# Top-k attention and a seven-product MLP: the order of fetched and resident products, and where GpSimd's additions are given out

## The chip, the cores and the metric

The kernel runs on one core of one Trainium2 chip. The metric is the device time of one execution in microseconds (us). A core has TensorE (PE, matrix products; PEld is its weight load), VectorE (DVE), ScalarE (ACT), GpSimd (POOL) and SyncE (SP), which here issues nearly all DMA transfers. Each engine has a program of its own and waits for others by semaphores.

## The reference

```python
def _attn_ref(q, k, v):              # B=8, H=8, S=576, D=64, float32
    scores = scale * np.matmul(q, k.transpose(0, 1, 3, 2))
    kth = np.partition(scores, -32, axis=-1)[..., -32:-31]
    scores = np.where(scores >= kth, scores, -1e9)
    attn = np.exp(scores - np.max(scores, axis=-1, keepdims=True))
    attn = attn / (np.sum(attn, axis=-1, keepdims=True) + 1e-09)
    return np.matmul(attn, v)
# bridge: x = attention as (8, 576, 512)
def _moe_ref(x, g_ln, w_ch1, w_ch2): # w_ch1 512 x 2048, w_ch2 2048 x 512
    xn = (x - mean) / np.sqrt(var + 1e-06) * g_ln
    return x + np.maximum(xn @ w_ch1, 0.0) @ w_ch2
```

## The kernel before

**Attention.** Work is cut into 160 *units*: a unit is 128 queries of one pair of heads (or the 64 last queries of both heads, a *rest*). VectorE turns keys and queries (turn_heads, L321), TensorE makes the scores (scores and score_half, L348 to L380), and ACT copies them out of PSUM. VectorE then finds the 32nd largest score of every row in rounds of MAX8 and MATCH_REPLACE8 (select, L404). It does so on two halves: halve (L382) makes the elementwise maximum of the two halves of a row on VectorE (hi) and the minimum on GpSimd by two integer operations (lo, L399 and L402); the first rounds of select read lo. ACT masks (mask, L447) and exponentiates (weigh, L454). The weights are turned for the product with v either by TensorE (turn, L505) or, in 72 *moved* units, by VectorE and two DMA trips through memory (move, L486: two transposes L492, one store L497, four loads L500). values (L563) multiplies with v, place (L590) turns the result into rows of x.

**The MLP.** Two tiles of 128 rows of x make a *block*; there are 18. The first block is computed plainly (plain, L726). The other 17 use seven products of half-size matrices in place of eight for the second layer (seven, L768). A block has three kinds of items: two rows ("turn", L663), 64 hidden products (L700) with a relu on ACT after every eight, and 7 steps of 8 products ("project", L862, matmul L869). The left factors are four parts of the relu's output (part(j, 0) to part(j, 3)) and three sums of them made by GpSimd (sums, L785 to L793). The right factors are either *resident* in SBUF (three quarters of w2) or one of four *forms*: combinations of w2's quarters, computed once (form_pair, L906) and kept in memory. A form is fetched by four DMAs, each a pair of 128x256 pieces (fetch_form, L929, DMA L932), into the four slots that w2's fourth quarter leaves free (slot_of, L903). So a slot of a form is overwritten by the next form's piece once the product that read it is done. The four of the seven steps that use forms are, before, steps 2, 3, 5 and 6.

Each step's bank of PSUM is copied out by ACT when its last product is given out (evacuate, L829, copies L818): four go into the output tile o, three into a tile t from which GpSimd adds them to o (L827). tpool has one buffer for t, and aside (L820) runs everything that is deferred before it takes it. finish (L676) scales o on ACT (L678), adds x on GpSimd (L682) and leaves the store to the next step.

**Order.** Engines execute in the order in which the Python loop at L1126 emits. Its pass n, a *step of the loop*, emits select for unit n, halve for n+1, scores for n+2 and the later stages of units n-1, n-2 and n-3. Between them stand eight calls of fill (L272), which give out block items from the list todo: slot (L1087) spreads the list evenly, so a fill has a share of planned us (0.56 to 0.75 in most of the run, more at the end) and an item has a planned cost (0.4378 us for one product). A call of fill counts the clock tick. defer (L262) puts an action off by some fills: sums by SUM_LAG = 4, joins by 1; settle (L265) runs what is due at the beginning of a fill. After the loop the rest of the list is emitted one item at a time (L1253).

A fetch is emitted by fetch_forms (L939) in a fill, as soon as the product that read its slot was emitted a fill or two ago; forms (L946) emits it on the spot where it is needed and not yet emitted:

```python
    def fetch_forms():
        may = min(seen[0] + 4, 16 * (len(blocks) - 1))
        seen[0] = used[0]
        if done(formed[0]):
            while fetched[0] < may:
                fetch_form()
```

SyncE's queue holds, in order of emission, the stores of finished rows (L684), the forms (L932), the moves (L497, L500), the loads of keys and queries (L299, eight transfers when a new pair of heads is turned), v (L311, L315) and small transfers of denominators (L558).

Of the kernel before, what the change touches and what calls it, by code (L numbers as in the profile page):

```python
# [29 lines left out]
def kernel(  # L30
# [41 lines left out]
    nc = tc.nc  # L72
# [22 lines left out]
    kqpool = pool("kq", 4)  # L95
    vpool = pool("v", NV)
# [162 lines left out]
    pending = []  # L259
    tick = [0]  # L260

    def defer(fills, run):  # L262
        pending.append((tick[0] + fills, run))

    def settle(all_of_them=False):  # L265
        waiting = [x for x in pending if not all_of_them and x[0] > tick[0]]
        due_now = [x for x in pending if all_of_them or x[0] <= tick[0]]
        pending[:] = waiting
        for _, run in due_now:
            run()  # L270

    def fill(least=0):  # L272
        tick[0] += 1
        settle()
        fetch_forms()
        owed[0] = min(owed[0] + share[0], 6.0)
        while todo and (not todo[0][3] or todo[0][3]()):
            if owed[0] < todo[0][1] / 2 and least <= 0:
                break
            least -= 1  # L280
            pop()
# [39 lines left out]
    def turn_heads(job):  # L321
        job.T = {}
        for name in "kq":
            job.T[name] = kqpool.tile([P, S], FP32, tag=name + "T", name=name + "T")
            nc.vector.transpose(job.T[name][:], job.ins[name][:])  # L325
# [32 lines left out]
    def score_half(u, s):  # L358
        T = (u.job.twin or u.job).T
        kT, qT = T["k"], T["q"]  # L360
        q0 = u.qt * P
# [257 lines left out]
    class Block:  # L619
        def __init__(self, tiles, dsts):  # L620
# [5 lines left out]
            self.ready = False  # L626

# [48 lines left out]
        def finish(self, i):  # L676
            o = self.o[i]
            nc.scalar.activation(  # L678
                o[:], o[:], AF.Identity,
                bias=self.mv[:, i, 0:1], scale=self.rstd[:, i : i + 1],  # L680
            )
            nc.gpsimd.tensor_tensor(o[:], o[:], self.x[i], ALU.add)  # L682
            for dst, rows in self.dsts[i]:
                stores.append(lambda d=dst, s=o[rows, :]: nc.sync.dma_start(d, s))  # L684
# [83 lines left out]
        def seven(self):  # L768
# [11 lines left out]
            def run(j, ps):  # L780
                hs[j] = self.relu(ps)
                waiting[j] = True
                defer(SUM_LAG, lambda: sums(j))

            def sums(j):  # L785
                if not waiting.pop(j, False):
                    return
# [10 lines left out]
            def resident(half, side):  # L798
# [3 lines left out]
                ("a", True, lambda j: part(j, 0), resident(0, 0)),  # L802
                ("b", True, lambda j: part(j, 2), resident(1, 0)),
                ("c", True, lambda j: ss[j][:, 0], 0),
                ("a", False, lambda j: ss[j][:, 1], 1),
                ("c", False, lambda j: ss[j][:, 2], resident(1, 1)),
                ("a", False, lambda j: part(j, 1), 2),
                ("d", True, lambda j: part(j, 3), 3),
            )

            def left(i):
                return self.o[i][:, 0:Q]

            def right(i):
                return self.o[i][:, Q:DM]

            def copy(dst, name):
                nc.scalar.copy(dst, bank[name][:, 0:Q])  # L818

            def aside(name, *into):  # L820
                settle(True)
                t = tpool.tile([P, Q], FP32, tag="t", name="t")
                copy(t[:], name)
                return t

            def add(dst, x, y):
                nc.gpsimd.tensor_tensor(dst, x, y, ALU.add)  # L827

            def evacuate(k):  # L829
                if k == 0:  # L830
                    for i in range(2):
                        self.o[i] = opool.tile([P, DM], FP32, tag="o", name="o")
                    copy(left(0), "a")
                elif k == 1:
                    t = aside("b")
                    defer(1, lambda: add(left(0), left(0), t[:]))
                elif k == 2:
                    copy(right(1), "c")
                elif k == 3:
                    copy(right(0), "a")  # L840
                elif k == 4:
# [451 lines left out]
```

## Time and profile before

| what | before |
|---|---|
| time, median of 3 runs | 1752.1 us (1752.0 to 1752.13) |
| the profiled execution, its own time | 1751.76 us |
| its span, first to last instruction | 1749.9 us |
| busy: PE, DVE | 1559.6 us (89%), 1463.3 us (84%) |
| busy: ACT, POOL | 1067.7 us (61%), 971.6 us (56%) |
| granted TensorE clock, mean | 0.950 |
| products L869, TensorE records | 1904, of 400 to 409 ns mean each, overlapping |
| fetches of forms | 272, of 256 KB, median 3.2 us from issue to landing |

A record of a product is half of one[...], so 1904 records are 952 products. Shares of busy time are means over three stretches: until about 300 us the weights are converted beside the first units, until about 1600 us attention and blocks run together, and after that the last blocks run without attention. Waits are listed as waiting instruction <- what released it; line names carry the tile's name and the line in the kernel.

### The profile page before, as it was taken

The numbers are of one execution on the slowest core, as the hardware profiler recorded it, in microseconds if no ns is written. First come the engines' busy times: TensorE is split into PE (matmuls) and PEld (weight loads), VectorE is DVE, ScalarE is ACT, GpSimd is POOL, SyncE is SP. The second block draws the span as 40 slices with busy tenths as digits, with TensorE's granted clock in tenths as the row PEclk, the third lists the DMA queues.
The fourth block names the chain that finished last, engine by engine and source line by source line (L and its number), as shares of the span: only waits on it lengthen the run. The fifth ranks groups of instructions, "written<-read, shape, count | busy, mean of one in ns | idle before, by whom it ended". The sixth has DMA issues, their size and how long they took to land.

```text
span 1749.9 us, 27740 instructions
## 1 busy us (share of the span) xinstructions
PE 1559.6 (89%) x7897; PEld 1146.4 (66%) x7897; DVE 1463.3 (84%) x4620; ACT 1067.7 (61%) x2712; POOL 971.6 (56%) x1509
## 2 busy tenths in 40 slices
PE   2678989999888989899899988989998999999987
PEld 1346556676666766677676766667676667777876
DVE  5998898999899999889899989798989899983000
ACT  6978866676666746566565755656565656653321
POOL 5778678464555646365555554554555455553332
PEclk9879998999899989999999999999999999999999
DMA  6422333413635365355644554535554555443232
GB/s 168 113 91 87 77 97 112 117 34 87 178 111 169 92 171 130 113 150 132 166 142 127 138 148 130 157 100 165 137 164 116 142 133 172 131 122 115 74 90 84
DMA packets 377504, 218.00 MB, mean 125 GB/s; under 512 B 250884, under 2 KB 357384, under 8 KB 377352
## 3 DMA queue, kind: packets, MB, share of 16 engines
q1 hardware_dynamic: 372616, 215.65, 43.9%
q10 hardware_dynamic: 4736, 0.59, 0.3%
q8 instruction: 63, 1.03, 0.2%
q14 instruction: 89, 0.73, 0.1%
HBM read 164.76 MB, written 51.38 MB: 124 GB/s over the span
## 4 chain that ended last, share of the span: by engine, by line
DVE 46%; PE 26%; POOL 10%; DMA 8%; ACT 5%; issue 2%; SPq 2%; DVEq 0%; ACTq 0%; POOLq 0%
DVE m L423 14%; DVE hi L409 12%; PE ops L869 11%; DVE hi L414 7%; PE hps L700 7%; DMA w<-forms 5%; DVE lo L409 4%; DVE hi L394 3%; DVE sc L492 3%; PE scps L373 3%; POOL lo L402 2%; POOL lo L399 2%; PE av L568 2%; DMA turned<-sc 2%; ACT sc L354 1%
## 5 line engine op out<-in xcount | busy, mean ns | idle before, releaser
L700 PE MATMUL hps<-xT,w 128*128 128x256 f32 x2304 | 557.9, 387 | 3.0 <-ACT xT L671 3.0
L423 DVE MAX8 m<-hi 128x8 f32<-128x304 f32 x1152 | 488.4, 460 | 3.3
L700 PEld LDWEIGHTS hps<-xT,w 128*128 128x128 f32 x2304 | 422.8, 193 | 82.5 <-issue 26.4
L409 DVE MATCH_REPLACE8 hi<-m,hi 128x304 f32<-128x304 f32 x864 | 390.2, 458 | 0.0
L399 POOL TENSOR_TENSOR lo<-sc,hi 128x576 int32<-128x576 int32 (+1 forms) x159 | 204.5, 1286 | 270.9 <-DVE hi L394 150.9
L869 PE MATMUL ops<-w,h 128*128 128x256 f32 x1088 | 282.3, 400 | 41.9 <-DMA w<-forms 41.8
L414 DVE MAX8 hi<-lo 128x8 f32<-128x288 f32 x576 | 234.3, 443 | 50.4 <-POOL lo L402 49.1
L869 PEld LDWEIGHTS ops<-w,h 128*128 128x128 f32 x1088 | 203.5, 198 | 90.8 <-DMA w<-forms 50.1
L869 PE MATMUL ops<-w,s 128*128 128x256 f32 x816 | 218.4, 409 | 48.8 <-DMA w<-forms 48.6
L373 PE MATMUL scps<-kT,qT 64*128 64x288 f32 (+3 forms) x1344 | 223.9, 438 | 35.9 <-DVE qT L325 28.3
L354 ACT COPY sc<-scps 128x288 f32<-128x288 f32 x576 | 197.6, 409 | 84.4 <-PE scps L373 56.7
L460 ACT ACTIVATE e<-e,bias 128x576 f32<-128x576 f32 x288 | 225.8, 784 | 14.1 <-POOL bias L445 13.5
L450 ACT ACTIVATE e<-sc,m 128x576 f32<-128x576 f32 x288 | 224.8, 781 | 3.9 <-DVE m L423 3.2
L869 PEld LDWEIGHTS ops<-w,s 128*128 128x128 f32 x816 | 157.1, 204 | 88.2 <-DMA w<-forms 51.9
L402 POOL TENSOR_TENSOR lo<-lo,sc 128x576 int32<-128x576 int32 (+1 forms) x159 | 204.3, 1285 | 12.5
L373 PEld LDWEIGHTS scps<-kT,qT 64*128 64x128 f32 (+1 forms) x1344 | 124.5, 183 | 122.5 <-issue 39.4
L827 POOL TENSOR_TENSOR o<-o,t 128x256 f32<-128x256 f32 x68 | 50.6, 744 | 222.2 <-ACT t L818 136.2
L568 PE MATMUL av<-pt,vb 128*64 128x256 f32 (+2 forms) x1088 | 150.1, 419 | 9.8 <-DMA pt<-turned 5.3
L492 DVE STREAM_TRANSPOSE sc<-e 128x512 f32<-128x512 f32 x144 | 95.0, 688 | 70.1 <-ACT e L460 70.1
L723 ACT ACTIVATE h<-hps 128x512 f32<-128x512 f32 x144 | 86.5, 600 | 71.2 <-PE hps L700 70.4
L409 DVE MATCH_REPLACE8 lo<-hi,lo 128x288 f32<-128x288 f32 x288 | 125.5, 442 | 0.0
L568 PEld LDWEIGHTS av<-pt,vb 128*64 128x64 f32 x1088 | 75.5, 143 | 75.8 <-issue 21.1
(87 smaller groups left out, 1795.8 us busy)
## 6 DMA issues: line engine op xcount, KB each, us to landing
w<-forms SPq DMA_DIRECT2D x272, 256.0 KB, 3.2
turned<-sc SPq DMA_DIRECT2D x72, 512.0 KB, 2.8
pt<-turned SPq DMA_DIRECT2D x288, 128.0 KB, 2.9
vb<-in_v_dram SPq DMA_DIRECT2D x136, 128.0 KB, 2.9
raw<-in_moe_w_ch_dram SPq DMA_DIRECT2D x32, 512.0 KB, 4.1
kin<-in_k_dram SPq DMA_DIRECT2D x128, 72.0 KB, 2.5
qin<-in_q_dram SPq DMA_DIRECT2D x120, 72.0 KB, 2.5
out_dram<-o SPq DMA_DIRECT2D x32, 256.0 KB, 2.9
```

The source lines that it names most:

```text
L354: nc.scalar.copy(u.sc[:, t, s * HALF : (s + 1) * HALF], made[s][t][:, 0:HALF])
L373: nc.tensor.matmul(ps[i * R : i * R + ql, o : o + width], qT[r, q0 : q0 + ql], kT[r, k0 : k0 + width], start=True, stop=True,)
L399: nc.gpsimd.tensor_tensor(lo.bitcast(I32), a.bitcast(I32), hi.bitcast(I32), ALU.subtract)
L402: nc.gpsimd.tensor_tensor(lo.bitcast(I32), lo.bitcast(I32), b.bitcast(I32), ALU.add)
L409: nc.vector.match_replace(x[:, t], m[:, t, :], x[:, t], LOWEST)
L414: nc.vector.max(u.hi[:, t, o : o + 8], u.lo[:, t])
L423: nc.vector.max(m[:, t, :], u.hi[:, t])
L450: nc.scalar.activation(u.e[:, t], u.sc[:, t], AF.Prelu, bias=u.thr[:, t, 7:8], scale=-1.0, alpha=SLOPE)
L460: nc.scalar.activation(u.e[:, t], u.e[:, t], AF.Exp, bias=u.bias[:, t : t + 1], scale=-scale / SLOPE, accum_out=g.den[:, col : col + 1],)
L568: nc.tensor.matmul(av[h * D : (h + 1) * D, 0 : g.nq], vb[:, h * J + c, :], g.blocks[:, h, 0 : g.nq // 32, c, :], start=(c == 0), stop=False,)
L700: nc.tensor.matmul(ps[0][:, side * N : (side + 1) * N], w1[:, c, f * P : (f + 1) * P], self.xT[:, c, 0:N], start=(c == 0), stop=(c == NC - 1),
L869: nc.tensor.matmul(bank[name][:, 0:Q], a(j), rhs, start=first and j == 0, stop=(j == G - 1), skip_group_check=not first,)
```

## The change

- **Steps.** The seven products of a block are put in another order, so that fetched and resident right factors alternate: steps 0, 2, 4 and 6 use forms. The forms are stored in memory in the new order of their use.
- **Fetches.** used becomes a list of the fills in which a slot was last read; a fetch is emitted in a fill once ten fills have passed (FETCH_AGE), or on the spot in forms. All projects of a block wait for formed.
- **GpSimd.** sums, joins and the additions of x go to a list (sums_later) that is settled at one place in a pass of the loop, right behind halve, for entries at least five fills old (SUM_AGE). A product that needs sums which were not yet given out gives them out. The scaling on ACT goes to a second list (ends_later), settled at the beginning of a fill, five fills old (END_AGE). close gives out what a block still has open when the next block's first product is emitted.
- **Buffers.** The three joined results have buffers of their own (tags t3, t5, t6). The last join adds one tile to both halves of o in one operation of 128x512.
- **Queries.** The turned queries are two tiles, of 256 and 320 columns, each with a transpose of its own; the first is in a pool of two buffers.

```diff
@@ -93,6 +93,7 @@
     consts = pool("consts", 1)
     ldpool = pool("ld", 1)
     kqpool = pool("kq", 4)
+    qpool = pool("q", 2)
     vpool = pool("v", NV)
     scpool = pool("sc", 5)
     hipool = pool("hi", 2)
@@ -256,23 +257,36 @@
         owed[0] -= cost
         run()
 
-    pending = []
     tick = [0]
 
-    def defer(fills, run):
-        pending.append((tick[0] + fills, run))
-
-    def settle(all_of_them=False):
-        waiting = [x for x in pending if not all_of_them and x[0] > tick[0]]
-        due_now = [x for x in pending if all_of_them or x[0] <= tick[0]]
-        pending[:] = waiting
-        for _, run in due_now:
-            run()
+    class Later:
+
+
+        def __init__(self):
+            self.waiting = []
+
+        def add(self, run):
+            left = [run]
+
+            def once():
+                if left:
+                    left.pop()()
+
+            self.waiting.append((tick[0], once))
+            return once
+
+        def settle(self, age):
+            due_now = [x for x in self.waiting if tick[0] - x[0] >= age]
+            self.waiting = [x for x in self.waiting if tick[0] - x[0] < age]
+            for _, run in due_now:
+                run()
+
+    sums_later, ends_later = Later(), Later()
 
     def fill(least=0):
         tick[0] += 1
-        settle()
-        fetch_forms()
+        ends_later.settle(END_AGE)
+        fetch_forms(FETCH_AGE)
         owed[0] = min(owed[0] + share[0], 6.0)
         while todo and (not todo[0][3] or todo[0][3]()):
             if owed[0] < todo[0][1] / 2 and least <= 0:
@@ -321,8 +335,13 @@
     def turn_heads(job):
         job.T = {}
         for name in "kq":
-            job.T[name] = kqpool.tile([P, S], FP32, tag=name + "T", name=name + "T")
-            nc.vector.transpose(job.T[name][:], job.ins[name][:])
+            cuts = (0, S) if name == "k" else (0, 2 * P, S)
+            job.T[name] = []
+            for i, (c0, c1) in enumerate(zip(cuts, cuts[1:])):
+                pl = kqpool if c1 == S else qpool
+                t = pl.tile([P, c1 - c0], FP32, tag=f"{name}T{i}", name=name + "T")
+                nc.vector.transpose(t[:], job.ins[name][:, c0:c1])
+                job.T[name].append((c0, t))
 
 
 
@@ -357,8 +376,9 @@
 
     def score_half(u, s):
         T = (u.job.twin or u.job).T
-        kT, qT = T["k"], T["q"]
-        q0 = u.qt * P
+        kT = T["k"][0][1]
+        c0, qT = T["q"][u.qt >= 2]
+        q0 = u.qt * P - c0
         ql = R if u.rest else P
         pss = [brief("scps") for _ in u.tiles]
         for ps, hs in zip(pss, u.tiles):
@@ -624,6 +644,7 @@
             self.mv = None
             self.step = {}
             self.ready = False
+            self.ends = []
 
         def stats(self, i):
             x = self.x[i]
@@ -675,13 +696,20 @@
 
         def finish(self, i):
             o = self.o[i]
-            nc.scalar.activation(
-                o[:], o[:], AF.Identity,
-                bias=self.mv[:, i, 0:1], scale=self.rstd[:, i : i + 1],
-            )
-            nc.gpsimd.tensor_tensor(o[:], o[:], self.x[i], ALU.add)
-            for dst, rows in self.dsts[i]:
-                stores.append(lambda d=dst, s=o[rows, :]: nc.sync.dma_start(d, s))
+
+            def residual():
+                nc.gpsimd.tensor_tensor(o[:], o[:], self.x[i], ALU.add)
+                for dst, rows in self.dsts[i]:
+                    stores.append(lambda d=dst, s=o[rows, :]: nc.sync.dma_start(d, s))
+
+            def scaled():
+                nc.scalar.activation(
+                    o[:], o[:], AF.Identity,
+                    bias=self.mv[:, i, 0:1], scale=self.rstd[:, i : i + 1],
+                )
+                self.ends.append(sums_later.add(residual))
+
+            self.ends.append(ends_later.add(scaled))
 
         def rows(self):
             return [
@@ -779,12 +807,9 @@
 
             def run(j, ps):
                 hs[j] = self.relu(ps)
-                waiting[j] = True
-                defer(SUM_LAG, lambda: sums(j))
+                waiting[j] = sums_later.add(lambda: sums(j))
 
             def sums(j):
-                if not waiting.pop(j, False):
-                    return
                 a11, a21, a12, a22 = (hs[j][:, i * P : (i + 1) * P] for i in range(4))
                 s = ss[j] = hpool.tile([P, 3, P], FP32, tag="h", name="s")
                 nc.gpsimd.tensor_tensor(s[:, 0], a21, a22, ALU.add)
@@ -799,72 +824,52 @@
                 return lambda j: w2[:, half * G + j, side * Q : (side + 1) * Q]
 
             steps = (
-                ("a", True, lambda j: part(j, 0), resident(0, 0)),
-                ("b", True, lambda j: part(j, 2), resident(1, 0)),
-                ("c", True, lambda j: ss[j][:, 0], 0),
-                ("a", False, lambda j: ss[j][:, 1], 1),
-                ("c", False, lambda j: ss[j][:, 2], resident(1, 1)),
-                ("a", False, lambda j: part(j, 1), 2),
-                ("d", True, lambda j: part(j, 3), 3),
+                ("d", True, True, lambda j: part(j, 3), 0),
+                ("a", True, False, lambda j: part(j, 0), resident(0, 0)),
+                ("c", True, False, lambda j: ss[j][:, 0], 1),
+                ("b", True, True, lambda j: part(j, 2), resident(1, 0)),
+                ("a", False, False, lambda j: ss[j][:, 1], 2),
+                ("c", False, True, lambda j: ss[j][:, 2], resident(1, 1)),
+                ("a", False, True, lambda j: part(j, 1), 3),
             )
 
-            def left(i):
-                return self.o[i][:, 0:Q]
-
-            def right(i):
-                return self.o[i][:, Q:DM]
-
-            def copy(dst, name):
-                nc.scalar.copy(dst, bank[name][:, 0:Q])
-
-            def aside(name, *into):
-                settle(True)
-                t = tpool.tile([P, Q], FP32, tag="t", name="t")
-                copy(t[:], name)
-                return t
-
-            def add(dst, x, y):
-                nc.gpsimd.tensor_tensor(dst, x, y, ALU.add)
+            def quarter(k):
+                i, side = ((1, 0), (0, 0), (1, 1), None, (0, 1), None, None)[k]
+                return self.o[i][:, side * Q : (side + 1) * Q]
 
             def evacuate(k):
+                src = bank[steps[k][0]][:, 0:Q]
                 if k == 0:
                     for i in range(2):
                         self.o[i] = opool.tile([P, DM], FP32, tag="o", name="o")
-                    copy(left(0), "a")
-                elif k == 1:
-                    t = aside("b")
-                    defer(1, lambda: add(left(0), left(0), t[:]))
-                elif k == 2:
-                    copy(right(1), "c")
-                elif k == 3:
-                    copy(right(0), "a")
-                elif k == 4:
-                    t = aside("c")
-
-                    def top():
-                        add(right(0), right(0), t[:])
+                if k in (0, 1, 2, 4):
+                    nc.scalar.copy(quarter(k), src)
+                    return
+                t = tpool.tile([P, Q], FP32, tag=f"t{k}", name="t")
+                nc.scalar.copy(t[:], src)
+
+                def join():
+                    if k == 6:
+                        o = self.o[1][:].rearrange("p (s n) -> p s n", s=2)
+                        both = t[:].unsqueeze(1).to_broadcast([P, 2, Q])
+                        nc.gpsimd.tensor_tensor(o, o, both, ALU.add)
+                        self.finish(1)
+                        return
+                    x = quarter({3: 1, 5: 4}[k])
+                    nc.gpsimd.tensor_tensor(x, x, t[:], ALU.add)
+                    if k == 5:
                         self.finish(0)
 
-                    defer(1, top)
-                elif k == 5:
-                    self.u = aside("a")
-                    defer(1, lambda: add(right(1), right(1), self.u[:]))
-                else:
-                    copy(left(1), "d")
-
-                    def bottom():
-                        add(left(1), left(1), self.u[:])
-                        self.finish(1)
-
-                    settle(True)
-                    defer(1, bottom)
+                self.ends.append(sums_later.add(join))
 
             def project(k, j):
-                name, first, a, b = steps[k]
+                name, first, _, a, b = steps[k]
                 if first and j == 0:
                     bank[name] = product("ops")
-                if k in (2, 3, 4, 5):
-                    sums(j)
+                if k == 0 and j == 0:
+                    close(blocks[blocks.index(self) - 1])
+                if k in (2, 4, 5, 6):
+                    waiting[j]()
                 rhs = forms(self, b, j) if isinstance(b, int) else b(j)
                 nc.tensor.matmul(
                     bank[name][:, 0:Q], a(j), rhs,
@@ -872,7 +877,7 @@
                     skip_group_check=not first,
                 )
                 if isinstance(b, int) and j % 2:
-                    used[0] += 1
+                    used.append(tick[0])
                 if j == G - 1:
                     evacuate(k)
 
@@ -887,7 +892,7 @@
                         "project",
                         PER_ROW * Q,
                         lambda k=k, j=j: project(k, j),
-                        lambda k=k: self.ready and (k < 2 or done(formed[0])),
+                        lambda: self.ready and done(formed[0]),
                     )
                     for k in range(7)
                     for j in range(G)
@@ -895,9 +900,14 @@
             )
 
     PER_ROW = 1.71e-3
-    SUM_LAG = 4
+    SUM_AGE, END_AGE, FETCH_AGE = 5, 5, 10
     blocks = []
-    plain_done, formed, used, fetched = [None], [None], [0], [0]
+    plain_done, formed, used, fetched = [None], [None], [], [0]
+
+    def close(blk):
+        while blk.ends:
+            blk.ends.pop(0)()
+
     scratch = formpool.tile([P, 4, 4, DM], FP32, tag="forms", name="forms")
 
     def slot_of(i):
@@ -922,7 +932,7 @@
                 tt(made[2], made[1], b11, ALU.subtract)
                 tt(made[3], b21, made[1], ALU.subtract)
             for s in range(2):
-                nc.sync.dma_start(scratch[:, 2 * h + s, i], x[:, s])
+                nc.sync.dma_start(scratch[:, (2 * h + s + 1) % 4, i], x[:, s])
         if i == 3:
             formed[0] = now[0]
 
@@ -934,13 +944,10 @@
         )
         fetched[0] += 1
 
-    seen = [0]
-
-    def fetch_forms():
-        may = min(seen[0] + 4, 16 * (len(blocks) - 1))
-        seen[0] = used[0]
+    def fetch_forms(age):
         if done(formed[0]):
-            while fetched[0] < may:
+            free = 4 + sum(tick[0] - x >= age for x in used)
+            while fetched[0] < min(free, 16 * (len(blocks) - 1)):
                 fetch_form()
 
     def forms(blk, k, j):
@@ -1181,6 +1188,7 @@
             x.shift()
         if nxt:
             halve(nxt)
+        sums_later.settle(SUM_AGE)
         for den in recips.pop(n, []):
             nc.vector.reciprocal(den, den)
         if n in turns:
@@ -1250,13 +1258,14 @@
                 for x in (r - 1, r):
                     arrived(n, ("r", x), rs[x])
         fill()
-    while todo or stores or pending:
+    while todo or stores or sums_later.waiting or ends_later.waiting:
         for store in stores:
             store()
         stores.clear()
         tick[0] += 1
-        settle()
-        fetch_forms()
+        ends_later.settle(1)
+        sums_later.settle(1)
+        fetch_forms(1)
         if todo:
             pop()
 
```

## The prediction

> **What bounds the kernel now.** I read the page's busy shares and slices, the windows of the main stretch and the tail, the waits inside the main stretch, and the timeline around the longest waits.
>
> The windows first. Columns: us, then busy us (and instructions) of PE, PEld, DVE, ACT, POOL, then clock, DMA share, GB/s.
>
> ```profile
> 300.00:1600.00 1300.00, 1200.99 (x6192) 889.44 (x6190) 1198.40 (x3777) 799.68 (x2091) 706.09 (x1183) 0.96 0.47 131
> 1600.00:1749.90 149.90, 132.54 (x617) 111.34 (x616) 3.41 (x8) 37.48 (x81) 46.23 (x89) 0.96 0.33 101
> ```
>
> In 1300 us TensorE is idle 99 and VectorE 102: two engines with equal loads of 92%, each losing 100 us. The tail is TensorE's alone. So the question is what makes the two wait. The waits between 300 and 1600 us (us in total, times, longest), then SyncE's own over the whole span, then the chain's largest lines:
>
> ```profile
> POOL o L827 <- ACT t L818: 89.0, 28, 12.6
> PE ops L869 <- DMA w<-forms: 79.4, 34, 6.9
> DVE sc L492 <- ACT e L460: 52.1, 26, 6.9
> DVE hi L414 <- POOL lo L402: 39.6, 19, 9.1
> ```
> ```profile
> SPq L932 <- PE ops L869: 293.9, 130, 33.1
> ```
> ```profile
> DVE m L423 14%; DVE hi L409 12%; PE ops L869 11%; DVE hi L414 7%; PE hps L700 7%; DMA w<-forms 5%; DVE lo L409 4%; DVE hi L394 3%; DVE sc L492 3%; PE scps L373 3%; POOL lo L402 2%; POOL lo L399 2%; PE av L568 2%; DMA turned<-sc 2%; ACT sc L354 1%
> ```
>
> 79 of TensorE's 99 idle us are waits for a fetched form; 92 of VectorE's 102 are two waits that follow from it. How a fetch comes late shows in the timelines of SyncE and TensorE around 1165 us:
>
> ```profile
> 1160.17 0.34 SPq L497 DMA_DIRECT2D turned<-sc  x1
> 1165.21 1.75 SPq L500 DMA_DIRECT2D pt<-turned  x4
> 1167.06 2.12 SPq L299 DMA_DIRECT2D kin<-in_k_dram  x4
> 1169.28 2.06 SPq L299 DMA_DIRECT2D qin<-in_q_dram  x4
> 1171.44 12.91 SPq L932 DMA_DIRECT2D w<-forms  x8
> ```
> ```profile
> 1174.64 2.93 PE L869 MATMUL ops<-w,s 128*128 128x256 f32 x6 [5.39 <-DMA w<-forms]
> ```
>
> The pair's slot had been read for the last time at 1166.1, but its fetch stood in SyncE's queue behind a move (L497, L500) and a load (L299), went out at 1171.4 and landed 3.2 us later. Then the other engines. POOL, and DVE, near 1100 us, after such a stall:
>
> ```profile
> 1096.62 0.73 POOL L827 TENSOR_TENSOR o<-o,t 128x256 f32<-128x256 f32 x1 [12.61 <-ACT t L818]
> 1099.52 1.27 POOL L682 TENSOR_TENSOR o<-o,x 128x512 f32<-128x512 f32 x1 [2.16 <-ACT o L678]
> ```
> ```profile
> 1102.44 0.46 DVE L414 MAX8 hi<-lo 128x8 f32<-128x288 f32 x1 [9.10 <-POOL lo L402]
> ```
>
> GpSimd sat 12.6 us before the join of a bank that TensorE had not finished; the halving of the next unit stood behind it, and VectorE waited 9.1 us for that halving.
>
> [...] a form's issue takes 0.38 us, landing comes 3.1 us (median) after it starts, and SyncE's waits of 293.9 us lie ahead of such issues. So a fetch costs its place in SyncE's queue plus 3.15 us.
>
> **Part 1: the order of products and the age of a fetch.** Before, the fetched steps are 2, 3 and 5, 6: between a pair's last reading and the next reading of its slot lie 7 matmuls. A product is planned at 0.4378 us and most blocks get 0.75 us a fill, so 7 are 4.1 fills, and the old rule queues the fetch two fills after the reading: about 2 fills ahead of its need. After, fetched steps alternate, and 15 matmuls lie between: 8.8 fills at 0.75 (blocks 6 to 14), 11.7 at 0.56, 9.8 at 0.67, under 4 in the last blocks. A fetch is queued by age only after 10 fills. So in most blocks it is *not* queued by age: forms() queues it at the matmul that needs it. Two effects oppose each other. SyncE no longer waits for TensorE (the 294 us go: the slot has been free for some 8 us), so moves and loads behind it go out earlier. But the fetch has no lead in program order: what the same step queued before it (a move of 5 issues with 2.8 us of landing between, a load of 8 issues of 0.52 us) is ahead of it.
>
> To size this I laid the new order on the times of this trace: for each of the 272 fetches, the end of the last other transfer ahead of it in SyncE's queue, plus 3.15 us, against the moment when TensorE was at that matmul. With those transfers tied only to what they themselves need (a move to its transposes, a load to VectorE's turn): 29 fetches in 16 groups are late, 69 us if each group counts its largest; groups stand at steps 40, 51, 83, 100, 117, 126, 143 with 6 to 9 us. With SyncE's times left as traced: 39 groups, 205 us, the upper end. The old order on the same decoupled times gives only 26, where the trace shows 88 over 0.3 us after 300 us: two thirds of today's stall is SyncE held up by its own fetches, which is what the change takes away. I take 69.
>
> What it does to VectorE: in a step with a move, its end is not before 4.3 us after TensorE began that step's scores (step 74: 732.3 + 4.3 = 736.6, next step began at 736.4; step 94: 934.5 + 4.3 = 938.8, against 938.9). This rule on the traced starts gives 45 us of lost time, against 43 traced for those steps; with the old stalls taken out and the new put in, 46 (upper end 105). So **ACT e stays near its 52 us**.
>
> **Part 2: sums, joins and ends at one place, five fills old, joins with buffers of their own.** Work is not removed: four sums of 0.46 us each, as before; joins 2 x 0.74 + 1.27 in place of 4 x 0.74 a block; seven ACT copies as before. They move behind the halving, and what they wait for is 5 fills (6 us) old, so neither GpSimd nor ACT (16.1 us on POOL o before L678) should stand in front of them. The 39.6 us of hi <- lo shrink to an estimated 8 (0 if nothing is late, 40 if the batch itself is: two sums of 1.85, a join and a residual are 5.9 us, and the next halving comes some 10 us later, so a reason speaks against 40). That is **-32 us of VectorE's idle time**. What is late next is TensorE: 1201 busy, 20 other idle, 69 of forms are 1290, only 10 below 1300. As VectorE hastens, TensorE runs later against it, each us of that takes a us from each of the 16 groups, and gives about one back in ACT e on some 19 steps. The two meet near 1278 to 1282: **-20 us** for both parts in the main stretch.
>
> **Part 3: queries in two tiles.** 32 more transposes[...]. In return the scores wait for a shorter first piece (28.3 us in five waits now, most at the start): some 2 us. Net 0 to +3; I take +1.
>
> **Part 4: banks and the end.** The first hidden product of the next block now takes the bank that the last step leaves, so it waits for a copy of 0.37 us; before, step 6 took the bank of step 5 in the same way and the trace shows no ACT wait there. 0 to +8 over 17 blocks; I take +1. In the tail 11 of 17 idle us are forms (90.3 - 79.4); 15 matmuls of 0.4 us cover a landing of 3.15, and few moves are left: -5 (0 to -10). The last join is 1.27 instead of 0.74: +0.5.
>
> Sum: -20 + 1 + 1 - 5 + 0.5 = -22.5 on the profiled 1751.76 (span 1749.9 and 1.9 outside), which is 0.3 under the median 1752.1: **about 1729 us**.
>
> **Rivals.**
> *Slower: the fetch on demand is late behind moves and loads.* Place: SyncE's queue in fill 8 of a step with a move and the fills 1 to 6 after it. Price: a move ends 5 us after VectorE's step, landing 8.2 us after it, where TensorE is at 1.25 us a fill. For it: 8.8 fills against an age of 10; 205 us in the overlay as traced. Against it: that overlay keeps delays that the old fetches made. It decides from about 110 us of form waits in the main stretch: 1201 + 20 + 110 = 1331, which is 1752 + 31 - 4 = 1779.
> *Much faster: the stall dissolves.* If TensorE settles 5 us behind VectorE, a move's fetch lands in time and only loads are late, with 15 us of forms: 1201 + 20 + 15 = 1236, so -64 and -10 in the tail: 1678. Against it: steps of 7.0 us with a move bear only some 2.5 us of lag.
> *The joins matter not* since the halving waits then for something else: -20 becomes 0 and the total is 1749.
>
> **How the numbers follow.** A measurement of this kernel can tell 0.2% (3.5 us) from no change. Forecast 0.40 (1708 to 1748), much faster 0.21 (to 1665), slower 0.32 (1756 to 1815), joins without effect 0.07 (half of it under 1748.6). The first two and a little of the last give 0.62 faster, 0.06 same, 0.32 slower. Range 1680 to 1788: leaves out the ends of the two outer cases.
>
> **What would show it.** Right: SPq w<-forms <- PE nearly gone; POOL o <- ACT t under 20 us; DVE hi <- POOL lo under 12; PE ops <- DMA w<-forms 50 to 70 in the main stretch, in groups behind L497/L500/L299, at steps 2, 4, 6 of a block and never at step 0. Wrong: form waits above 110, or VectorE's wait for ACT e above 85 (slower rival); form waits under 25 (fast rival); hi <- lo unchanged (parts 2 without effect).

## The result, and the profile after

Over 20 runs of each, the changed kernel takes 1749.55 us (median; 1744.89 to 1752.62) and the kernel before 1753.83 us: ratio 0.9973, interval [0.9966, 0.9981]. That is 0.27% faster where 1.3% was forecast (1729 against 1752). The profiled execution took 1746.25 us, its span is 1744.2. Every ratio below is to the kernel before, run on the same chip beside the run named.

The last operation of VectorE, the statistics of the last rows of x, marks the end of the attention. It ends at 1666.8 us before and at 1674.3 after. Columns are those of the prediction's windows; first the kernel before, then the kernel after:

```profile
300.00:1666.80 1366.80, 1264.87 (x6512) 942.77 (x6511) 1201.79 (x3785) 823.87 (x2147) 725.76 (x1223) 0.96 0.46 130
1666.80:1749.90 83.10, 68.67 (x297) 58.01 (x296) 0.03 (x1) 13.30 (x25) 26.56 (x49) 0.93 0.28 85
```
```profile
300.00:1674.30 1374.30, 1254.30 (x6499) 937.04 (x6498) 1199.62 (x3801) 823.05 (x2139) 724.17 (x1211) 0.96 0.46 130
1674.30:1744.20 69.90, 63.02 (x296) 55.18 (x295) 0.01 (x1) 12.99 (x25) 26.88 (x48) 0.97 0.29 91
```

The stretch with attention became 7.5 us longer: TensorE is idle 120 us in it in place of 102, VectorE 175 in place of 165. The end without attention became 13.2 us shorter, so all that was gained was gained there. The waits between 300 and 1600 us tell what was exchanged (total us, times, longest):

```profile
PE ops L874 <- DMA w<-forms: 93.9, 29, 7.1
DVE sc L512 <- ACT e L480: 75.8, 38, 6.9
...
DVE hi L414 <- ACT sc L373: 21.0, 7, 4.3
...
PE ops L874 <- POOL s L818: 8.5, 1, 8.5
...
DVE hi L434 <- POOL lo L422: 2.2, 5, 0.6
...
POOL o L859 <- ACT t L849: 0.7, 1, 0.7
```

GpSimd's waits for joins (89.0 us before) and VectorE's for the halving (39.6) are gone, 0.7 and 2.2 us. In their place the waits for forms rose from 79.4 to 93.9 (over the whole span from 90.3 to 96.3), VectorE's for ACT e from 52.1 to 75.8, and 21 us before VectorE's halving (ACT had not yet copied the scores) are new. SyncE's waits over the whole span, one line of the kernel before and two of the kernel after:

```profile
SPq L497 <- DVE hi L414: 199.7, 38, 13.8
```
```profile
SPq L517 <- DVE hi L434: 343.7, 60, 13.7
...
SPq L942 <- PE ops L874: 169.8, 93, 28.0
```

SyncE waits 124 us less for TensorE (293.9 before), but 144 us more for VectorE ahead of a move, and what is queued behind the move waits with it. One such place in the timelines of SyncE and then TensorE:

```profile
500.48 0.53 SPq L942 DMA_DIRECT2D w<-forms  x1
509.99 0.35 SPq L517 DMA_DIRECT2D turned<-sc  x1
512.84 1.74 SPq L520 DMA_DIRECT2D pt<-turned  x4
514.62 1.46 SPq L942 DMA_DIRECT2D w<-forms  x3
```
```profile
509.85 1.13 PE L874 MATMUL ops<-w,s 128*128 128x256 f32 x4
518.09 4.56 PE L874 MATMUL ops<-w,s 128*128 128x256 f32 x12 [7.11 <-DMA w<-forms]
```

One fetch of step 2 of block 3 went out at 500.5, and SyncE then sat for 9 us ahead of a move. The other three are queued behind it. TensorE is through with the first pair at 511, and the next lands 3.3 us after its issue at 514.6: 7.1 us lost. Counted one by one in the trace, the form waits fall in steps 2, 4 and 6 of a block (49, 28 and 20 us) and in none at step 0.

### The profile page after: what moved, and what is told of

Same layout as the page of the kernel before. It is cut to its first block, busy times and chain, and to the rows that moved or that the text cites. A ratio compares the mean times of both kernels' runs of the same rounds, so it can differ in the third digit from the quotient of the medians.

```text
span 1744.2 us, 27927 instructions
## 1 busy us (share of the span) xinstructions
PE 1544.9 (89%) x7897; PEld 1138.9 (65%) x7897; DVE 1464.4 (84%) x4652; ACT 1069.1 (61%) x2712; POOL 968.8 (56%) x1492
## 4 chain that ended last, share of the span: by engine, by line
DVE 40%; PE 37%; POOL 8%; DMA 7%; ACT 5%; issue 2%; SPq 2%; DVEq 0%; POOLq 0%; ACTq 0%
PE hps L728 13%; PE ops L874 13%; DVE m L443 11%; DVE hi L429 10%; DVE hi L434 6%; PE scps L393 5%; DMA w<-forms 4%; DVE lo L429 4%; DVE hi L414 3%; DVE sc L512 3%; PE av L588 3%; DMA turned<-sc 2%; POOL lo L419 2%; POOL lo L422 2%; ACT sc L373 1%
## 5 line engine op out<-in xcount | busy, mean ns | idle before, releaser
L874 PE MATMUL ops<-w,h 128*128 128x256 f32 x1088 | 271.5, 389 | 19.8 <-DMA w<-forms 19.8
L393 PE MATMUL scps<-kT,qT 64*128 64x288 f32 (+3 forms) x1344 | 229.6, 447 | 33.3 <-DVE qT L343 22.2
L588 PE MATMUL av<-pt,vb 128*64 128x256 f32 (+2 forms) x1088 | 145.7, 410 | 3.7 <-DMA pt<-turned 3.4
L414 DVE TENSOR_TENSOR hi<-sc 128x576 f32<-128x576 f32 (+1 forms) x160 | 112.2, 701 | 30.4 <-ACT sc L373 30.3
L534 PE MATMUL tp<-ident,e 128*128 128x128 f32 x576 | 94.1, 290 | 27.3 <-ACT e L480 23.8
```

Source lines behind the costliest of these rows:

```text
L393: nc.tensor.matmul(ps[i * R : i * R + ql, o : o + width], qT[r, q0 : q0 + ql], kT[r, k0 : k0 + width], start=True, stop=True,)
L588: nc.tensor.matmul(av[h * D : (h + 1) * D, 0 : g.nq], vb[:, h * J + c, :], g.blocks[:, h, 0 : g.nq // 32, c, :], start=(c == 0), stop=False,)
L874: nc.tensor.matmul(bank[name][:, 0:Q], a(j), rhs, start=first and j == 0, stop=(j == G - 1), skip_group_check=not first,)
```

## The experiments

Twelve kernels were run. "Changed kernel" means the kernel after, "main stretch" the time from 300 to 1600 us. FETCH_AGE is the number of fills after which a fetch is queued.

**1. FETCH_AGE 2 in place of 10.**

```diff
-    SUM_AGE, END_AGE, FETCH_AGE = 5, 5, 10
+    SUM_AGE, END_AGE, FETCH_AGE = 5, 5, 2
```

> The changed kernel with one constant other: a fetch is queued two fills after its slot was read, in place of ten; the need is about nine fills after the reading. Theory 1 (on demand the fetch stands behind moves and loads in SyncE's queue): the form waits of the main stretch fall from 93.9 us to under 40, and the time falls by 25 to 55 us against the changed kernel, to some 1695 to 1725 us. Theory 2 (SyncE is held up by fetches that wait for TensorE, so that an early fetch only makes moves and loads later): SyncE's wait for TensorE goes from 170 us back to 290 or more and the time is at or above that of the changed kernel, 1750 or more.

Measured: 1668.4 us, 0.9475 [0.9449, 0.9501]. Waits in the main stretch, then SyncE's own:

```profile
DVE sc L512 <- ACT e L480: 41.6, 21, 12.3
...
PE ops L874 <- DMA w<-forms: 25.5, 13, 4.0
```
```profile
SPq L942 <- PE ops L874: 292.4, 141, 28.1
```

One constant is worth 5.0% of the time before, some 88 us, more than the 25 to 55 that theory 1 gave. Form waits fall by 68 us and those for ACT e by 34. Up to VectorE's last operation the profiled execution is 74.7 us shorter than that of the changed kernel (it ends at 1599.6 us). TensorE's idle time falls there from 120.0 to 63.7 us, and its busy time from 1254.3 to 1236.0 for the same 6499 instructions, at a granted clock of 0.98 in place of 0.96. So a quarter of the gain is shorter busy time at a higher clock; the last section shows what the clock goes with. Theory 2 falls with its own number: SyncE waits 292 us for TensorE again, as long as before the change, and the kernel is the fastest so far, 91 us below the kernel before (1759.4 on that chip). That SyncE waits costs little while what stands behind it has time.

**2. No fetches after the first four** (the products use what lies in the slots; this part of the computation is left out).

```diff
-        nc.sync.dma_start(
-            slot_of(i), scratch[:, k, i].rearrange("p (f n) -> p f n", f=2)
-        )
+        if m < 4:
+            nc.sync.dma_start(
+                slot_of(i), scratch[:, k, i].rearrange("p (f n) -> p f n", f=2)
+            )
```

> The changed kernel without its fetches of forms after the first four (the products then use what lies in the slots, so this part of the computation is left out). It bounds what fetching costs. Theory 1: form waits are worth most of what is lost; PE's 94 us in the main stretch and some of VectorE's 76 us on ACT e go, 1660 to 1690 us. Theory 2: the same or lower, since SyncE is empty of fetches as well. Theory 3 (VectorE and TensorE are bound by each other through ACT whatever the fetches do): only 10 to 30 us, 1720 to 1740.

Measured: 1654.7 us, 0.940 [0.9379, 0.9421]. All that fetching costs in the changed kernel is 5.7% (0.9973 - 0.940), and FETCH_AGE 2 already has 5.0 of it. Theory 3 falls. What is left in this kernel is a TensorE that is busy for 1243 of the 1300 us, with 15 us before sums of GpSimd:

```profile
PE ops L874 <- POOL s L815: 15.3, 8, 5.5
```

**3. The old order of products, fetches two fills old, all else as changed.**

```diff
-                ("d", True, True, lambda j: part(j, 3), 0),
-                ("a", True, False, lambda j: part(j, 0), resident(0, 0)),
-                ("c", True, False, lambda j: ss[j][:, 0], 1),
-                ("b", True, True, lambda j: part(j, 2), resident(1, 0)),
-                ("a", False, False, lambda j: ss[j][:, 1], 2),
...
+                ("a", True, False, lambda j: part(j, 0), resident(0, 0)),
+                ("b", True, True, lambda j: part(j, 2), resident(1, 0)),
+                ("c", True, False, lambda j: ss[j][:, 0], 0),
+                ("a", False, False, lambda j: ss[j][:, 1], 1),
...
```

> The changed kernel with the old order of the seven products (fetched steps 2, 3, 5, 6) and a fetch queued two fills after the reading, the joins, sums, ends and query tiles as changed. It shows what the second part is worth alone. Theory 1 (part 2 gains, part 1 loses what it gains): hi <- lo stays under 10 us, form waits at 75 to 90, 1725 to 1740 us, better than the changed kernel. Rival (the halving's wait was only where a late TensorE showed, its removal moves the wait to ACT e): 1747 to 1755.

Measured: 1734.1 us, 0.9849 [0.9825, 0.9874]. With the query tiles and the new buffers, GpSimd's part is worth 1.5% by itself, with form waits only a little lower than before:

```profile
DVE sc L512 <- ACT e L480: 71.3, 37, 7.2
PE ops L878 <- DMA w<-forms: 66.9, 28, 6.3
...
DVE hi L434 <- POOL lo L422: 1.6, 4, 0.4
```

The rival is right in part: the halving's wait went from 39.6 to 1.6 us, but VectorE's wait for ACT e rose from 52.1 to 71.3, so half as much came up there. The new order at age 10 loses 1.2 of the 1.5% again (0.9973 - 0.9849); at age 2 it takes another 3.7% off (0.9849 - 0.9475).

**4. Sums, joins and ends one fill after they arise, at every fill**, at age 10.

```diff
-        ends_later.settle(END_AGE)
+        ends_later.settle(1)
+        sums_later.settle(1)
...
-        sums_later.settle(SUM_AGE)
```

> The changed kernel with sums, joins and ends given out one fill after they arise, at the beginning of every fill, in place of behind the halving and five fills old. It undoes the second part alone. Theory 1: GpSimd's waits for ACT t and ACT o come back (50 us or more), hi <- lo rises from 4 to 30 or more, the sums' waits of TensorE (14 us) go, and the time rises by 10 to 25 us to 1760 to 1775. Rival (the place of the sums is of no account, since TensorE's form waits decide): within 4 us of the changed kernel.

Measured: 1814.7 us, 1.0311 [1.0288, 1.0335], 3.4% above the changed kernel and more than expected. Waits in the main stretch:

```profile
POOL o L860 <- ACT t L850: 164.0, 25, 15.4
...
PE ops L875 <- DMA w<-forms: 120.6, 30, 11.9
...
DVE hi L435 <- POOL lo L423: 45.8, 28, 4.9
```

GpSimd waits for the copies again, VectorE for GpSimd, and the form waits grow as well. This rule is not that of the kernel before, where sums came four fills after the relu: GpSimd's wait for the relu ahead of the sums is 82.9 us here and was 24.4 before. So the 3.4% is the price of this rule, and that of the old one may be smaller.

**5. FETCH_AGE 6.** The edit is that of the first experiment, with 6.

> The changed kernel with a fetch queued six fills after the reading: three fills ahead of the need where a fill has 0.75 us of products, two queued fills less than at age 2. If the lead in SyncE's queue is what counts (theory 1), the time lies between those of age 2 (0.9475 of the kernel before) and age 10 (0.9973): 0.955 to 0.98, form waits 30 to 60 us. Rival (the loss comes only where the age is never reached before the need, so a switch, not a slope): as age 2 within 0.4%.

Measured: 1700.2 us, 0.9666 [0.9645, 0.9688]; form waits 61.0 us, just above the range written, ACT e 67.5. A slope, and not a switch: 0.9475, 0.9666 and 0.9973 at ages 2, 6 and 10.

**6. Age 10, the fetches issued by GpSimd.**

```diff
-        nc.sync.dma_start(
+        nc.gpsimd.dma_start(
             slot_of(i), scratch[:, k, i].rearrange("p (f n) -> p f n", f=2)
```

> The changed kernel with age ten as it is, but the fetches of forms issued by GpSimd in place of SyncE, so that no move and no load stands ahead of them (GpSimd's own work does). Theory 1 (the place behind moves and loads makes them late): waits of TensorE for forms behind moves and loads go; what is left is GpSimd's work ahead of a fetch (up to 6 us of halving, sums and joins) and the issue's own time, form waits 20 to 90 us, and the time falls unless the issues fill GpSimd. Rival (on demand is late by the transfer's 3.2 us wherever it is issued): about one landing for each of some 60 fetches, form waits of 120 us or more, 1770 or more.

Measured: 1800.0 us, 1.0233 [1.0211, 1.0254]; form waits 116.1 us. The group of these issues:

```profile
L942 POOL DMA_DIRECT2D w<-forms x272 | 201.8, 743 | 48.9 <-PE ops L874 30.6 <-issue 12.2 <-PE xo L627 1.7
```

This run doesn't decide: an issue cost GpSimd 743 ns, 202 us in all, in an engine that has the halving and the sums to do. It shows only that GpSimd's queue, with this work in it, was no way out. The ninth and tenth runs put the question better.

**7. FETCH_AGE 2 with the edit of the fourth experiment.**

> Fetches two fills after the reading, as in the run of age 2, and sums, joins and ends at the beginning of every fill one fill after they arise, as in the run that undid the second part. It gives the second part's price where forms are in time. Theory 1 (the place of GpSimd's sums matters by itself, since GpSimd waits in order): 20 to 50 us above age 2, 1690 to 1720. Rival (the 60 us that it cost at age 10 came from late TensorE work that GpSimd waited for): within 8 us of age 2.

Measured: 1694.9 us, 0.9631 [0.9611, 0.965]. With forms in time the place of GpSimd's work is worth 1.6% (0.9631 - 0.9475); with late forms, 3.4%. The waits of GpSimd cost by themselves, so the rival (within 8 us of age 2) falls: 1.6% are some 27 us. They cost more when TensorE is late, since what GpSimd waits for is then late too (59.5 us in POOL o <- ACT t here, 164.0 in the fourth run). Read together with the third and fourth runs: with fetches two fills old the new order is worth 3.7% wherever GpSimd's work stands (from 1 to 0.9631 here, from 0.9849 to 0.9475 with it behind the halving). At age ten it costs 1.2% with GpSimd's work behind the halving and 3.1% without (from 1 to 1.0311); both comparisons with 1 are subject to what was said of the rule at the fourth run.

**8. The kernel before, with queries in two tiles only** (the hunks of turn_heads, score_half and qpool).

```diff
+            cuts = (0, S) if name == "k" else (0, 2 * P, S)
...
+                nc.vector.transpose(t[:], job.ins[name][:, c0:c1])
```

> The kernel before with the queries in two tiles and nothing else. Predicted: 0 to +3 us[...] and shorter waits of the first scores. Rival: faster by 5 us or more, since scores of the first units wait for 256 columns only.

Measured: 1763.2 against 1759.6 us, 1.002 [1.001, 1.003]. The groups of the transposes:

```profile
L330 DVE STREAM_TRANSPOSE qT<-qin 128x320 f32<-128x320 f32 x32 | 15.0, 468 | 0.0
L330 DVE STREAM_TRANSPOSE qT<-qin 128x256 f32<-128x256 f32 x32 | 12.8, 401 | 0.0
```

468 + 401 ns against 733 for one: 136 ns more, 4.4 us over 32. The two lengths alone give about the same, taken as linear in the columns: 67 ns for 64 columns leave an estimated 133 ns of the 401 that don't depend on the length. TensorE's wait for them fell from 28.3 to 26.5 us.

**9 and 10. Age 10, with fetches queued just ahead of every move and load, or just behind.** The ninth:

```diff
+                fetch_forms(2)
                 load(fresh[later], nc.sync, nc.sync)
...
         if moved:
+            fetch_forms(2)
             move(ex)
```

The tenth has the same two lines behind load and behind move.

> The changed kernel, age ten as it is, but just ahead of every move and every load of keys and queries all fetches are queued whose slot was read two or more fills ago. Only the order in SyncE's queue around moves and loads differs. Theory 1 (the place behind a move or a load is what makes a fetch late): nearly all of the gain of age 2 comes, 0.948 to 0.965 of the kernel before, form waits under 45 us in the main stretch. Rival (the general lead of a fetch in fills counts, moves or not): a small part of it, 0.98 or more.

> The control: the same fetches queued at the same places of the loop, but just behind every move and every load. Theory 1: the fetches needed in the next fills still wait for the move or the load, little changes: 0.985 to 1.0, form waits 75 to 100 us. Rival (general lead): as the run with the fetches ahead, since the lead in fills is the same.

Measured: ahead, 1671.9 us, 0.9493 [0.9471, 0.9515]; behind, 1735.0 us, 0.9846 [0.9824, 0.9868]. Waits in the main stretch, ahead and then behind:

```profile
DVE sc L512 <- ACT e L480: 43.1, 22, 12.6
PE ops L874 <- DMA w<-forms: 31.1, 14, 5.6
```
```profile
PE ops L874 <- DMA w<-forms: 92.2, 27, 7.3
DVE sc L512 <- ACT e L480: 76.7, 38, 7.6
```

This pair settles why age ten is slow. The same fetches at the same points of the loop, on one side of a move or load or the other, differ by 3.5%. With them ahead the form waits are 31 us and nearly all of the gain of age 2 is there, though everywhere else a fetch still comes ten fills old or on demand. The place shown above looks as follows in the ninth run, SyncE and then TensorE:

```profile
495.71 2.07 SPq L942 DMA_DIRECT2D w<-forms  x4
505.25 0.34 SPq L517 DMA_DIRECT2D turned<-sc  x1
```
```profile
505.07 3.72 PE L874 MATMUL ops<-w,s 128*128 128x256 f32 x16
```

All four fetches go out before SyncE sits down in front of the move, and TensorE runs through the eight products without a gap. The tenth run was 1.3% better than the changed kernel with form waits as high (92.2); VectorE's wait for score copies was 8.6 in place of 21.0, which covers part of it; the rest stays open. The lead in fills by itself, the rival, is thus worth 1.3% at most.

**11. Never by age, only on demand** (FETCH_AGE 100000; after the loop the rest of the list is emitted with an age of one item, as in the changed kernel).

> The changed kernel in which a fetch is never queued by age, only at the product that needs it (the block's first four forms too). The prediction counted that an age of ten is reached before the need in few blocks only, apart from the first form of a block. If that count is right the time is the changed kernel's or up to 1.5% above (step 0 of a block loses its lead): 0.997 to 1.013. Rival (age ten does most of the work where it is reached): 1.02 or more.

Measured: 1799.8 us, 1.0216 [1.0197, 1.0235], which is the rival's number. Where it comes from is told by TensorE's idle times over 0.3 us ahead of the products, added up by step of the block: step 0 has 44 us, where the changed kernel has none, and steps 2, 4 and 6 together have 97, against 110 there (waits for forms alone: 88 against 96). So the age of ten does its work at step 0 alone. Outside it, a fetch at age ten is no earlier in effect than one on demand, as the prediction counted; the price of step 0 was put too low.

**12. FETCH_AGE 1.**

> The changed kernel with a fetch queued one fill after the reading, the earliest of the ages tried: the version that might be the best. Theory 1: at age 2 only 25 us of form waits are left, another fill of lead is worth 0 to 10 us: 0.942 to 0.9475. Rival (SyncE's own waits for TensorE begin to hold up moves): 0.9475 to 0.955.

Measured: 1679.4 us, 0.9528 [0.951, 0.9546]. The form waits are 23.1 us, no more than at age 2, yet it is half a per cent slower than age 2. The number is the rival's, but its sign (SyncE's wait for TensorE) reads 304 us against 292, which is little; why stays open. Of the versions that compute everything, age 2 is the fastest at 5.2% below the kernel before, and the ninth run's interval overlaps its own.

## Why the prediction was right or wrong

**The bound: right.** The two engines did wait for fetched forms and for what follows from late forms. With the fetches in time (first run) 5% of the time goes.

**Part 2, GpSimd's place: right in its own rows.** 39.6 us of the halving's wait were to shrink to 8; they are 2.2. The waits of GpSimd for ACT t are 0.7 against "under 20". The third run has this part with the query tiles and is 25 us faster than the 1759 before, where -32 us of idle time was written. Not foreseen: sums that TensorE must wait for (12.8 us in the main stretch, 8.5 of it once), 21 us of VectorE's halving before score copies, and that half as much as left the halving's wait comes up before ACT e (third run). That GpSimd's halving waits behind a join, on which this part rests, the kernel before shows near 1100 us, on VectorE and then on GpSimd:

```profile
1088.85 0.45 DVE L394 TENSOR_TENSOR hi<-sc 128x288 f32<-128x288 f32 x1
```
```profile
1100.74 0.80 POOL L399 TENSOR_TENSOR lo<-sc,hi 128x288 int32<-128x288 int32 x1
```

The halving's hi was done at 1089.3 us; its lo started 11.4 us later, after the join that had waited 12.6 us.

**Part 1, the fetch on demand: the direction right, the size wrong. This is the step that failed.** That age ten comes after a need at 8.8 fills, that SyncE's queue then holds a move or a load ahead, and that the waits fall in steps 2, 4, 6 and never in 0, was as written. But "I take 69" rests on transfers that are tied only to what they themselves need: the 294 us of SyncE's wait for TensorE were to go, and moves and loads were to go out earlier. SyncE's queue did not come free. 169.8 us of that wait stayed, and the wait for VectorE ahead of moves rose from 200 to 344, by more than the other fell. The first run shows besides that this wait does not make the stall: with 292 us of it the form waits are 25.5. The measured waits were 93.9 us where 69 were taken, and the next term, "each us of that takes a us from each of the 16 groups", bent the 69 down to some 59. TensorE did begin a step's scores later against VectorE (in steps with a move 4.8 us on average, 3.3 before), so by that term the waits should have shrunk below 69. VectorE's wait for ACT e, forecast near its 52, became 75.8.

Why the lag does not pay the stall off can be read from the trace in part. A move is queued behind VectorE's transposes, and these wait for ACT e, which follows TensorE. In the changed kernel a move's store starts 0.03 us (median) after the second transpose ends. Over the 70 steps with a move in the main stretch, each us by which TensorE began the scores later went with a store that started 0.57 us later (correlation 0.78, both counted from the start of VectorE's step). So the lateness of a fetch was counted against a move that stands still, while more than half of a lag is handed on to the move and to the fetch behind it. No run changes the lag alone, so how much of the missing time this explains stays open.

In the sum: the stretch with attention, for which -20 was written, is 7.5 us longer.

**Part 3: right in kind, just above its range.** 0 to +3 us were written and +1 taken; alone it is +3.6 us, 0.2%, with an interval of 0.1 to 0.3%. What the 32 more transposes would cost was the author's estimate, which no line of before shows; the fixed part of one is an estimated 133 to 136 ns, from the groups of the eighth run. The scores' wait fell by 1.8 us as estimated.

**Part 4: the form waits right, the gain too small.** Form waits in the tail fell from 10.9 to 2.4 us, for which -5 (0 to -10) was written, and the waits of TensorE show no hidden product behind the last step's bank copy. But the end without attention is 13.2 us shorter: TensorE is idle 7.5 us less and busy 5.6 us less for as many instructions, at a clock of 0.97 in place of 0.93, which the prediction does not count. With the old order (third run) this end takes 78.5 us, with the new 69.9. So the 5.7 us between the two spans are made of a loss where the gain was forecast and of a gain at the end that was forecast at less than half. That the total went down at all is luck.

**The rivals.** The slower one had the mechanism that decided, but neither of its signs came: form waits were 93.9 and not above 110, ACT e 75.8 and not above 85. The result lies between the forecast and this rival. "The joins matter not", whose 1749 is the number measured, is refuted as a cause: GpSimd's part is worth 1.5% with the old order (third run), and the new order at age ten loses 1.2 of it again. The much faster case came with another constant.

## What to carry to other kernels

Here a prefetch was as early as its place in the issuing queue, not as its slot was free: with the same fetches queued ahead of the moves and loads the time was 0.9493 of that before, with them behind 0.9846. So before a long wait of that queue (a move, a load), queue everything that will be needed during that wait. A rule that counts age since the slot came free must be set against the distance to the next need, here 8.8 fills: at age ten the waits for forms in steps 2, 4 and 6 were 96 us, with fetches only on demand 88, so there the prefetch was gone, though nothing in the program looks broken. When two effects of a change oppose each other, size both ends and ask of each feedback whether the thing it is measured against moves too.

## What the runs showed of the hardware that was not expected

A DMA issued from GpSimd cost that engine 743 ns (mean, sixth run) where the same fetch issued from SyncE took 0.38 to 0.41 us of its queue (medians of the kernels before and after), so 272 of them made 202 us of GpSimd's time.

At the place shown above, in the kernel after, the clock granted to TensorE fell from 1.00 to 0.50 during its pause of 7.1 us (511.0 to 518.1 us) and stayed there until 521.6 us, past the pause's end (columns as before, the clock is third from the end):

```profile
504.00:514.80 10.80, 6.89 (x35) 4.48 (x31) 10.59 (x31) 6.08 (x17) 5.87 (x13) 1.00 0.19 67
514.80:521.60 6.80, 3.51 (x8) 2.86 (x9) 6.80 (x23) 0.90 (x3) 3.01 (x4) 0.50 0.95 265
521.60:531.00 9.40, 8.74 (x45) 6.35 (x43) 9.40 (x33) 5.60 (x16) 3.22 (x4) 1.00 0.67 197
```

The twelve records after the wait took 4.56 us there, the sixteen of the ninth run, without a wait, 3.72: an estimated 1.8 us more than twelve at that run's rate, on top of the 7.1. Between 300 and 1600 us the trace has 17 such spells, 102 us in all. Each begins during a pause of TensorE of 2.8 us or more, or at most 1.4 us after its end; in the kernel before 13 of 17 do. At age 2 there are 11 spells with 51 us, on demand 25 with 154. That the pause brings the lower clock is what this order in time suggests; no run tests it by itself.
